# Loading half of k through another queue in fp32, moving the first loads forward, and transposing exponentials as 32-bit words

## The chip, the core and the metric

The kernel runs on one NeuronCore of a Trainium2 chip. A core has a matrix engine (TensorE, PE in the profile, with its weight loads as PEld), a vector engine (VectorE, DVE), a scalar engine (ScalarE, ACT), a general engine (GpSimd, POOL) and a sequencer that issues transfers (SyncE, SP). Each engine works through its own instructions in order; semaphores tie the engines together. Transfers between device memory and the on-chip memory SBUF are issued from SP, ACT or POOL and carried out by 16 DMA engines; matmul results land in eight banks of PSUM. The metric is the device time of one execution in microseconds, as the median of several runs.

## The reference, cut to what matters

```python
def sm_attn(qq, kk, vv):                      # per batch and head
    s = scale * (qq @ kk.T); s = s - s.max(-1)
    a = exp(s); a = a / (a.sum(-1) + 1e-9)
    return a @ vv
p_packed = sm_attn(p, k, v)                   # 32 x 576 scores, per head
x = sm_attn(q, p_packed, p_packed)            # 576 x 32 scores, per head
x = x as [batch, 576, 8 heads * 64]           # then, per batch:
W = (x @ w_q) @ (x @ w_k).T / 8               # 576 x 576
out = relu(W @ x) @ w_out
```

There are 8 batches, 8 heads, 576 positions, 64 channels a head and 32 packed queries p. All tensors are fp32 in device memory; the kernel computes its matmuls in bf16.

## The kernel before, in words

The whole work is unrolled for the eight batches. The string `ORDER` is a list of steps written out by hand, and each engine gets its instructions in the order in which the steps stand there. A step is written `name.batch.part=banks@engine`: `S1.2=2,3,6,7` is the first score product of batch 2 into those PSUM banks, `X1.2.0@A` is an exponential on ACT. `WARM.n` issues n matmuls of 128x512 on a zeroed tile whose result nobody reads; they stand in PE's own order like any other matmul.

For each batch the steps are these. `LD` loads k, q and v; POOL issues these loads, and they turn fp32 into bf16 on the way. `KT` and `QV` (DVE, line 246) transpose k and q in 32x32 blocks of 32-bit words, so that two neighbouring bf16 numbers move as one word. `S1` forms the scores of p with k (lines 282 and 292), `X1` their exponentials (lines 300 and 303), `TE` transposes them on DVE (batches 2 to 7 only; for batches 0 and 1, listed in `DIAG`, S1 gives them already turned), `PV` multiplies them with v and a column of ones (line 323), `RC` and `PP` divide, `PT` transposes the result. `S2`, `X2`, `RS`, `RR`, `AM`, `AT`, `AE` are the second attention, `QK` to `MX` and `MR` the mixing, `RL` the ReLU, `OT` the output product (line 548), `OE` its copy out of PSUM and `ST` the store.

The head of the kernel is what the change touches most. `LD.E0` and `LD.E1` load p of batches 0 and 1 in fp32 (`p32`), one from SP and one from ACT; `EC` on ACT casts both to bf16 in one copy, `EX` on DVE transposes them, and four `PB` copies place them in a block-diagonal operand for S1 of batch 0; three run on DVE, `PB.0.0` on POOL. `LD.F` loads the first 128 rows of the output weights in fp32 from SP into an output buffer that is free then, and `FC` casts them on ACT into `wout`; `LD.O` later brings the other 384 rows through POOL, casting on the way. `LD.h0` and `LD.g0` load the second and the first half of k of batch 0 through POOL. `SET.v` fills the columns of ones beside v, and the loads of v stand behind them.

POOL's loads have eight semaphores to report their landing, used in turn. A load that takes up a semaphore again waits until the load eight places before it has landed, so at most eight are under way.

The exponentials of a batch from 2 on live in `e1T`, which X1 fills in two calls. The call for part cc covers two PSUM banks (the two values of x) of 288 scores; TE transposes the same part in 32x32 blocks of bf16 numbers.

Of the kernel before, what the change touches and what calls it, by code (L numbers as in the profile page):

```python
# [63 lines left out]
def kernel(  # L64
# [64 lines left out]
    def copy(eng, o, i):  # L129
        if eng == "A":  # L130
            nc.scalar.activation(o, i, COPY)  # L131
        elif eng == "P":
            nc.gpsimd.tensor_copy(o, i)
        else:
            nc.vector.tensor_copy(o, i)
# [20 lines left out]

    def load(x, eng):
        a, b = x[0], x[1:]
        if a in "gh":
            i = "gh".index(a)  # L160
            nc.gpsimd.dma_start(k_in[0][:, i], pairs(k, 0)[:, i])
        elif a == "P":
            c = int(b)
            src = p.rearrange("b (i c) (y l) d -> c (b i) y (l d)", i=2, y=2)
            nc.gpsimd.dma_start(pbf[quarter(c)], src[c])
        elif a == "E":
            b = int(b)
            src = p[b].rearrange("(i c) l d -> (c l) i d", i=2)
            (nc.sync if eng == "S" else nc.scalar).dma_start(p32[:, 2 * b:2 * b + 2], src)
        elif a == "W":  # L170
            w = (moe_w_k, moe_w_q)[int(b)].rearrange("(i c j e) m -> (c j) i (e m)", i=2, c=4, e=2)
            nc.gpsimd.dma_start(wqk[:, :, int(b)].rearrange("a i e m -> a i (e m)"), w)
        elif a == "O":
            nc.gpsimd.dma_start(wout[:, 1:], moe_w_out[P:].rearrange("(j a) n -> a j n", a=P))
        elif a == "F":
            nc.sync.dma_start(T["o"][0][:, 0], moe_w_out[0:P])
        elif a == "v":
            b = int(b)
            for i in range(2):
                src = v[b, 4 * i:4 * i + 4].rearrange("c (g r) d -> g c (r d)", r=R)  # L180
                nc.gpsimd.dma_start(v_bufs[b % NL][halves(i), 0:7:2], src)  # L181
        elif a == "k":
            b = int(b)
            nc.gpsimd.dma_start(k_in[b % NL], pairs(k, b))
        elif a == "r" or x in ("q0", "q7"):
            b, i = int(b), int(a == "q")
            nc.gpsimd.dma_start(q_in[b % NL][:, i], pairs(q, b)[:, i])
        else:
            b = int(b)
            nc.gpsimd.dma_start(q_in[b % NL], pairs(q, b))  # L190
# [54 lines left out]
    def blocks(o, i):  # L245
        nc.vector.transpose(o, i)  # L246
# [26 lines left out]
    def S1(b, eng, bk):  # L273
        kT = T["kT", b]
        if b in DIAG:
            z, dz = bk[0], bk[1] - bk[0]
            ps = ps_all[:, z]
            T["s1", b] = bass.AP(ps.tensor, ps.offset, [ps.ap[0], [dz * 512, 3], [1, 384]])
            for r in range(R):
                for e in range(2):  # L280
                    for i in range(2):
                        nc.tensor.matmul(ps_all[halves(i), bk[r // 3], r % 3 * P:(r % 3 + 1) * P],  # L282
                                         kT[:, i, r, :, e],
                                         pblk[:, 2 * b + i, :, :, e].rearrange("a c l -> a (c l)"),
                                         start=e == 0, stop=e == 1, skip_group_check=True)
            return
        T["s1", b] = [ps_all[:, n:n + 2, 0:NT] for n in (bk[0], bk[2])]
        for e in range(2):
            for z in range(4):
                for c in range(4):  # L290
                    i, gh = (c + z) // 2 % 2, (c + z) % 2
                    nc.tensor.matmul(T["s1", b][c // 2][quarter(2 * i + gh), c % 2],  # L292
                                     pT[quarter(c), 2 * b + i, :, e],
                                     kT[quarter(c), i, :, gh * 32:(gh + 1) * 32, e],
                                     start=e == 0, stop=e == 1)

    def X1(b, cc, eng, bk):
        if b in DIAG:
            e1 = new("e1", b, [P, R, C, 2, L], bufs=NE)
            nc.scalar.activation(e1.rearrange("a (z r) c x l -> a z (r c x l)", z=3), T["s1", b], EXP, scale=scale)  # L300
            return
        e1T = new("e1T", b, [P, C, 2, NT], bufs=1)
        nc.scalar.activation(e1T[:, cc], T["s1", b][cc], EXP, scale=scale)  # L303

    def TE(b, cc, eng, bk):
        e1 = new("e1", b, [P, R, C, 2, L], bufs=NE)
        if cc == 2:
            blocks(e1.rearrange("a r c x l -> a (c x) r l"),
                   T["e1T", b].rearrange("a c x (r m) -> a (c x) r m", r=R))
            return  # L310
        blocks(e1[:, :, cc].rearrange("a r x l -> a x r l"),
               T["e1T", b][:, cc].rearrange("a x (r m) -> a x r m", r=R))

    def PV(b, c, eng, bk=None):
        if bk:
            T["pv", b] = ps_all[:, bk[0]:bk[1] + 1, 0:3 * Dh]
        vt = v_bufs[b % NL]
        for n in range(5 * c, min(5 * c + 5, R)):
            for cc in range(C):
                for i in range(2):  # L320
                    rhs = vt[halves(i), 4 * cc:4 * cc + 3, n * Dh:(n + 1) * Dh]
                    lhsT = T["e1", b][halves(i), n, cc].rearrange("a x l -> a (x l)")
                    nc.tensor.matmul(T["pv", b][halves(cc), i], lhsT, rhs, start=n == 0,  # L323
                                     stop=n == R - 1, skip_group_check=True)

# [274 lines left out]
    steps = dict(EC=EC, FC=FC, EX=EX, PX=PX, PB=PB, KT=KT, S1=S1, X1=X1, TE=TE, PV=PV, RC=RC, PP=PP,  # L600
                 PT=PT, QK=QK, QKE=QKE, QD=QD, QV=QV, S2=S2, X2=X2, HA=HA, RS=RS, RR=RR, AM=AM,
                 AT=AT, AE=AE, WKQ=WKQ, WE=WE, GM=GM, GE=GE, Y=Y, YE=YE, MX=MX, MR=MR, RL=RL, RLF=RLF,
                 RLR=RLR, OT=OT, OE=OE, OEF=OEF, ST=ST, STF=STF,
# [49 lines left out]
```

## Time and profile before

| | us |
|---|---|
| median of three runs (lowest, highest) | 107.18 (106.27, 107.47) |
| the profiled execution | 107.46 |
| its span in the trace | 105.4 |
| PE busy in the span | 95.4 |
| DVE busy | 78.2 |
| ACT busy | 65.4 |
| POOL busy | 47.0 |

The span is the time from the first to the last instruction that the profiler saw; some 2.1 us of the execution lie around it. Busy times are sums over instructions, and PE's contain the WARM matmuls. The granted clock of PE was 0.995 of full speed over the span. A group's row in the profile gives line, engine, operation, output and inputs, shapes and count, then the busy time of the group and the mean of one in ns, then the idle time ahead of it and what ended that. A row of the timeline begins with the start and the length of a group of equal instructions in us. The DMA share is the mean busy share of the 16 DMA engines; overlapping packets let it pass 1, and GB/s counts the bytes written.

### The profile page before, as it was taken

What the parts mean: (1) busy time and instruction counts of PE and PEld (TensorE: products, weight loads), DVE (VectorE), ACT (ScalarE), POOL (GpSimd) and SP (SyncE); (2) the same over time, 40 slices, a digit from 0 to 9 for tenths busy, and PEclk for the clock granted to TensorE, in tenths of its full rate; (3) what the DMA queues carried; (4) which work ended last, traced back from release to release, by engine and by line L of the source; (5) the groups of instructions that cost most, each with busy time, mean ns of one, the idle gap of its engine ahead of it and who ended that gap; (6) DMA issues with size and microseconds to landing.
All of it is one profiled execution on the core that took longest, in us unless ns stands there. A gap on an engine that the chain in (4) does not pass through costs nothing.

```text
span 105.4 us, 3620 instructions
## 1 busy us (share of the span) xinstructions
PE 95.4 (91%) x1550; PEld 52.2 (50%) x1550; DVE 78.2 (74%) x150; ACT 65.4 (62%) x108; POOL 47.0 (45%) x76
## 2 busy tenths in 40 slices
PE   3992999798999999999999999999999999999930
PEld 1341645464644654654547536575466654643410
DVE  3615083999798989888898998989997989768000
ACT  5210405043657957879989898598997885556640
POOL 5899540843874226221046459915747019000000
PEclk9999999999999999999999999999999999999997
DMA  2999999999999999999999999999999999868693
GB/s 71 190 185 209 209 202 204 212 207 212 205 211 213 205 207 213 212 211 207 213 213 206 219 200 210 214 206 214 238 342 390 402 401 392 359 239 341 247 339 121
DMA packets 14095, 25.00 MB, mean 237 GB/s; under 512 B 2176, under 2 KB 6912, under 8 KB 14080
## 3 DMA queue, kind: packets, MB, share of 16 engines
q0 software_dynamic: 10176, 15.99, 81.6%
q1 hardware_dynamic: 3488, 8.59, 21.1%
q8 instruction: 12, 0.20, 0.7%
q10 hardware_dynamic: 416, 0.20, 0.7%
q14 instruction: 3, 0.02, 0.1%
HBM read 30.28 MB, written 9.44 MB: 377 GB/s over the span
## 4 chain that ended last, share of the span: by engine, by line
PE 59%; DVE 13%; DMA 10%; POOL 7%; ACT 3%; issue 3%; ACTq 0%; POOLq 0%; DVEq 0%
PE ps L548 26%; DMA k_sb<-in_k_dram 10%; DVE rs L402 4%; PE ps L381 4%; PE ps L323 4%; PE ps L620 4%; PE ps L500 3%; PE ps L427 3%; PE ps L454 3%; PE ps L449 3%; DVE kT L246 2%; DVE a L413 2%; PE ps L475 2%; POOL a L413 2%; PE ps L344 2%
## 5 line engine op out<-in xcount | busy, mean ns | idle before, releaser
L548 PE MATMUL ps<-wout,relu 128*128 128x512 bf16 x124 | 30.7, 380 | 0.0
L620 PE MATMUL ps<-o 128*128 128x512 bf16 x82 | 21.9, 405 | 1.8 <-DVE o L138 1.8
L413 POOL TENSOR_TENSOR a<-e,rr 128x1024 bf16<-128x1024 f32 (+2 forms) x10 | 12.5, 1266 | 18.5 <-DVE rr L407 18.5
L131 ACT ACTIVATE o<-ps 128x1024 f32<-128x1024 f32 (+2 forms) x18 | 15.2, 858 | 4.7 <-PE ps L548 4.7
L548 PEld LDWEIGHTS <-relu 128*128 128x128 bf16 x124 | 10.8, 98 | 11.9 <-issue 2.2
L386 ACT ACTIVATE e<-ps 128x256 f32<-128x256 f32 (+2 forms) x19 | 11.1, 620 | 7.8 <-PE ps L381 7.5
L246 DVE STREAM_TRANSPOSE kT<-k_sb 128x1152 uint32<-128x1152 uint32 (+1 forms) x9 | 11.1, 1235 | 4.6 <-DMA k_sb<-in_k_dram 4.6
L620 PEld LDWEIGHTS <-o 128*128 128x128 bf16 x82 | 7.6, 103 | 10.7 <-issue 2.7
L181 POOL DMA_DIRECT2D v_sb<-in_v_dram x16 | 10.1, 634 | 5.7 <-DMA k_sb<-in_k_dram 2.1
L402 DVE TENSOR_REDUCE rs<-e 128x16 f32<-128x512 f32 (+2 forms) x13 | 10.9, 844 | 1.4 <-ACT e L386 1.2
L511 ACT ACTIVATE relu<-ps 128x1024 bf16<-128x1024 f32 (+1 forms) x12 | 11.1, 954 | 0.6 <-PE ps L506 0.6
L246 DVE STREAM_TRANSPOSE qT<-q_sb 128x1152 uint32<-128x1152 uint32 (+1 forms) x10 | 11.1, 1107 | 0.0
L246 DVE STREAM_TRANSPOSE e<-e1T 128x576 bf16<-128x576 bf16 x12 | 8.7, 745 | 0.6 <-ACT e1T L303 0.6
L131 ACT ACTIVATE wkq<-ps 128x448 bf16<-128x448 f32 (+1 forms) x10 | 7.1, 732 | 2.9 <-PE ps L454 2.2
L303 ACT ACTIVATE e1T<-ps 128x576 bf16<-128x576 f32 x12 | 7.4, 650 | 1.6 <-PE ps L292 1.6
L323 PE MATMUL ps<-v_sb,e 64*64 64x192 bf16 x288 | 7.5, 245 | 0.0
L300 ACT ACTIVATE e<-ps 128x1152 bf16<-128x1152 f32 x2 | 2.3, 1132 | 8.4 <-PE ps L282 8.4
L381 PEld LDWEIGHTS <-qT 64*128 64x128 bf16 x320 | 5.5, 94 | 2.8 <-DVE qT L246 1.6
L323 PEld LDWEIGHTS <-e 64*64 64x64 bf16 x288 | 5.8, 106 | 1.9 <-ACT e L300 1.0
L454 PE MATMUL ps<-aT,pqk 128*128 128x256 bf16 (+1 forms) x48 | 6.8, 246 | 0.0
L381 PE MATMUL ps<-ppT,qT 64*128 64x64 bf16 x320 | 6.4, 190 | 0.3 <-DVE qT L246 0.2
L190 POOL DMA_DIRECT2D q_sb<-in_q_dram x6 | 4.3, 714 | 4.7 <-DMA q_sb<-in_q_dram 2.7
(78 smaller groups left out, 144.4 us busy)
## 6 DMA issues: line engine op xcount, KB each, us to landing
out_dram<-o SPq DMA_DIRECT2D x11, 512.0 KB, 5.3
v_sb<-in_v_dram POOLq DMA_DIRECT2D x16, 288.0 KB, 10.6
k_sb<-in_k_dram POOLq DMA_DIRECT2D x7, 576.0 KB, 12.0
q_sb<-in_q_dram POOLq DMA_DIRECT2D x6, 576.0 KB, 13.7
out_dram<-o SPq DMA_DIRECT2D x5, 256.0 KB, 2.4
q_sb<-in_q_dram POOLq DMA_DIRECT2D x4, 288.0 KB, 9.9
out_dram<-o POOLq DMA_DIRECT2D x2, 512.0 KB, 13.7
out_dram<-orem SPq DMA_DIRECT2D x4, 256.0 KB, 5.1
```

The costliest lines, as they stand in the source:

```text
L131: nc.scalar.activation(o, i, COPY)
L181: nc.gpsimd.dma_start(v_bufs[b % NL][halves(i), 0:7:2], src)
L246: nc.vector.transpose(o, i)
L323: nc.tensor.matmul(T["pv", b][halves(cc), i], lhsT, rhs, start=n == 0, stop=n == R - 1, skip_group_check=True)
L381: nc.tensor.matmul(ps[:, y, t - t0, i], lhsT, rhs, start=e == 0, stop=e == 1)
L386: nc.scalar.activation(e2[:, t0:t1].rearrange("a t (i y n) -> a y (t i) n", i=2, y=2), T["s2", b, c].rearrange("a y t i n -> a y (t i) n") ...
L402: nc.vector.tensor_reduce(rs[:, t0 * H:t1 * H], src, axis=AX, op=ADD)
L413: e.tensor_tensor(a2[:, t0:t1].rearrange("a t i (u l) -> a (t i u) l", l=L), e2v(b, c), T["rr", b][:, t0 * H:t1 * H].to_broadcast((P, (t1 ...
L454: nc.tensor.matmul(o, pqk[:, i, Dl:], aT[:, i, c0:c1], start=i == 0, stop=i == 1)
L511: nc.scalar.activation(o, i, RELU)
L548: nc.tensor.matmul(ps, lhsT, wout[:, j, :], start=j == 0, stop=j == NJ - 1)
L620: nc.tensor.matmul(ps, warm[:, 0:P], warm, start=True, stop=True)
```

## The change

The change has three parts.

The first half of k of batch 0 no longer goes through POOL. It is loaded in fp32 by SP (`LD.H`), as SP's first transfer, into the output buffer where the output weights' rows lay before, and ACT casts it into `k_sb` (`HC`, in `FC`'s place). E0 moves to ACT's queue and E1 to SP's, behind H. POOL begins with the second half of k (`LD.g0`), then v and q of batch 0; the column of ones for v of batch 0 is set by DVE at the very start, and that for batch 3 by POOL after these loads.

The output weights come in one POOL transfer of all 512 rows, at the place of the former `LD.O`; `LD.F` and `FC` are gone.

The exponentials of batches 2 to 7 are stored with the two values of c next to each other, so that a pair is one 32-bit word. S1 writes its four score blocks to the same four banks, two of them exchanged; X1 reads the two banks of its part alternately, one element of each, and writes the pairs; TE transposes 288 words a call instead of 576 bf16 numbers; PV reads its weights with a step of two.

```diff
-LD.E0@S LD.E1@A LD.F@S SET.pz0@V SET.aT0@V SET.warm@V SET.tab@A EC@A FC@A EX@V SET.v1@V SET.idf@V PB.0.2@V LD.h0
-SET.v3@P LD.g0 SET.v0@P LD.v0 LD.q0 SET.mask@P PB.0.0@P PB.0.3@V KT.0.1@V KT.0.0@V PB.0.1@V
+LD.H@S LD.E0@A LD.E1@S SET.v0@V SET.pz0@V SET.aT0@V SET.warm@V SET.tab@A EC@A HC@A EX@V SET.v1@V SET.idf@V PB.0.2@V
+LD.g0 LD.v0 LD.q0 SET.v3@P SET.mask@P PB.0.0@P PB.0.3@V KT.0.1@V KT.0.0@V PB.0.1@V
...
-        if a in "gh":
-            i = "gh".index(a)
-            nc.gpsimd.dma_start(k_in[0][:, i], pairs(k, 0)[:, i])
+        if a == "g":
+            nc.gpsimd.dma_start(k_in[0][:, 1], pairs(k, 0)[:, 1])
...
-            nc.gpsimd.dma_start(wout[:, 1:], moe_w_out[P:].rearrange("(j a) n -> a j n", a=P))
-        elif a == "F":
-            nc.sync.dma_start(T["o"][0][:, 0], moe_w_out[0:P])
+            nc.gpsimd.dma_start(wout, moe_w_out.rearrange("(j a) n -> a j n", a=P))
+        elif a == "H":
+            nc.sync.dma_start(h32, pairs(k, 0)[:, 0])
...
+    h32 = T["o"][0].rearrange("a t n -> a (t n)")[:, 0:RQ * Dh]
...
-    def FC(eng, bk):
-        copy(eng, wout[:, 0], T["o"][0][:, 0])
+    def HC(eng, bk):
+        copy(eng, k_in[0][:, 0], h32)
...
-                    nc.tensor.matmul(T["s1", b][c // 2][quarter(2 * i + gh), c % 2],
+                    nc.tensor.matmul(T["s1", b][c % 2][quarter(2 * i + gh), c // 2],
...
-        e1T = new("e1T", b, [P, C, 2, NT], bufs=1)
-        nc.scalar.activation(e1T[:, cc], T["s1", b][cc], EXP, scale=scale)
+        e1T = new("e1T", b, [P, 2, NT, C], bufs=1)
+        nc.scalar.activation(e1T[:, x], T["s1", b][x].rearrange("a c m -> a m c"), EXP, scale=scale)
...
-        blocks(e1[:, :, cc].rearrange("a r x l -> a x r l"),
-               T["e1T", b][:, cc].rearrange("a x (r m) -> a x r m", r=R))
+    def TE(b, x, eng, bk):
+        e1 = new("e1", b, [P, R, C, 2, L], bufs=NE).rearrange("a r c x l -> a r (c x l)").bitcast(u32)
+        blocks(e1[:, :, x * L:(x + 1) * L],
+               T["e1T", b][:, x].rearrange("a m c -> a (m c)").bitcast(u32).rearrange("a (r m) -> a r m", r=R))
+
+    def e1_of(b, i, n, cc):
+        e1 = T["e1", b][halves(i), n]
+        if b in DIAG:
+            return e1[:, cc].rearrange("a x l -> a (x l)")
+        return e1.rearrange("a c x l -> a (c x l)").rearrange("a (m c) -> a m c", c=C)[:, :, cc]
...
-                    lhsT = T["e1", b][halves(i), n, cc].rearrange("a x l -> a (x l)")
+                    lhsT = e1_of(b, i, n, cc)
```

More of the change, by code (lines that the diff above doesn't have):

```diff
@@ L295, in S1, with X1 @@
                                      start=e == 0, stop=e == 1)
-    def X1(b, cc, eng, bk):
+    def X1(b, x, eng, bk):
         if b in DIAG:
@@ L301, in X1 @@
             return
-        e1T = new("e1T", b, [P, C, 2, NT], bufs=1)
[L303 to L310, printed above, removed]
-        blocks(e1[:, :, cc].rearrange("a r x l -> a x r l"),
-               T["e1T", b][:, cc].rearrange("a x (r m) -> a x r m", r=R))
+        e1T = new("e1T", b, [P, 2, NT, C], bufs=1)
[9 more added lines that the diff above has]
+        return e1.rearrange("a c x l -> a (c x l)").rearrange("a (m c) -> a m c", c=C)[:, :, cc]
     def PV(b, c, eng, bk=None):
@@ L598, in STF @@
         q.dma_start(orows(b)[:, :, t * D:(t + 1) * D], T["o", b][:, t])
-    steps = dict(EC=EC, FC=FC, EX=EX, PX=PX, PB=PB, KT=KT, S1=S1, X1=X1, TE=TE, PV=PV, RC=RC, PP=PP,
+    steps = dict(EC=EC, HC=HC, EX=EX, PX=PX, PB=PB, KT=KT, S1=S1, X1=X1, TE=TE, PV=PV, RC=RC, PP=PP,
                  PT=PT, QK=QK, QKE=QKE, QD=QD, QV=QV, S2=S2, X2=X2, HA=HA, RS=RS, RR=RR, AM=AM,
```

## The prediction

> **What bounds the kernel now.** I read the windows first, to see which engine is full at what time.
>
> ```profile
> span 105.4 us, 3620 instructions
> ...
> 10.00:20.00 10.00, 9.06 (x144) 4.93 (x146) 4.61 (x11) 2.49 (x4) 4.52 (x9) 1.00 1.19 206
> 20.00:30.00 10.00, 9.70 (x185) 6.18 (x182) 9.18 (x25) 4.51 (x9) 5.83 (x11) 1.00 1.14 209
> 30.00:38.00 8.00, 7.70 (x162) 4.08 (x160) 7.48 (x17) 5.40 (x11) 4.11 (x6) 1.00 1.15 208
> 46.00:58.00 12.00, 11.50 (x244) 7.00 (x245) 10.40 (x18) 10.95 (x19) 3.64 (x5) 1.00 1.14 211
> 58.00:70.00 12.00, 12.00 (x256) 6.63 (x256) 11.60 (x20) 9.76 (x15) 7.96 (x12) 1.00 1.15 211
> 10.00:101.20 91.20, 89.08 (x1529) 49.80 (x1529) 73.94 (x139) 62.43 (x103) 38.68 (x55) 1.00 1.08 247
> ```
>
> The columns are PE, weight loads, DVE, ACT, POOL, clock, DMA share, GB/s. From 10 us to 101.2 us PE is busy 89.08 of 91.20 us, so it stands still for 2.1 us in all: 0.94 in 10 to 20, 0.30 in 20 to 30, 0.30 in 30 to 38, 0.50 in 46 to 58, and none in 58 to 70. Part of this work is filler (the WARM steps), but the filler is a fixed number of matmuls in PE's own order, so PE cannot run ahead of it. The time is therefore the start of the first real matmul, plus a fixed PE load, plus 2.1 us of standstill, plus a tail that the change leaves alone. Only the start and the standstill can shrink. Next, PE's waits and the chain:
>
> ```profile
> PE ps L282 <- DVE o L135: 1.9, 1, 1.9
> PE ps L282 <- DVE kT L246: 0.6, 1, 0.6
> PE ps L344 <- DVE ppT L246: 0.3, 1, 0.3
> ```
>
> ```profile
> 7.61 10.76 DMA k_sb<-in_k_dram
> 18.39 1.38 DVE kT L246
> ```
>
> The 1.9 us is the wait ahead of the first S1. The 0.6 and 0.3 both hang on one landing: k of batch 1, issued at 7.61, releases DVE at 18.39; DVE then works without a break until the 0.3 us wait. The head in order of time:
>
> ```profile
> 1.29 0.73 POOL L161 DMA_DIRECT2D k_sb<-in_k_dram  x1 [0.82 <-POOLq L637]
> ...
> 1.83 6.37 PE L620 MATMUL ps<-o 128*128 128x512 bf16 x21 [1.83 <-DVE o L138]
> ...
> 3.11 0.42 ACT L131 ACTIVATE o<-o 128x256 bf16<-128x256 f32 x1 [0.34 <-DMA o<-in_p_dram]
> ...
> 3.94 0.54 DVE L214 MEMSET v_sb<- 128x576 uint32 x1
> ...
> 4.66 0.62 DVE L135 COPY o<-o 32x256 bf16<-32x256 bf16 x2
> ...
> 5.13 0.63 ACT L131 ACTIVATE wout<-o 128x512 bf16<-128x512 f32 x1 [1.60 <-DMA o<-in_moe_w_out_dram]
> ...
> 7.60 0.78 DVE L246 STREAM_TRANSPOSE kT<-k_sb 128x576 uint32<-128x576 uint32 x1 [2.33 <-DMA k_sb<-in_k_dram]
> 8.98 0.78 DVE L246 STREAM_TRANSPOSE kT<-k_sb 128x576 uint32<-128x576 uint32 x1 [0.60 <-DMA k_sb<-in_k_dram]
> 9.79 0.22 DVE L135 COPY o<-o 32x256 bf16<-32x256 bf16 x1
> 10.06 1.24 PE L282 MATMUL ps<-o,kT 128*64 128x128 bf16 x36 [1.86 <-DVE o L135]
> ```
>
> The first load on POOL (second half of k) releases DVE at 7.60, the second (first half) at 8.98, so one 288 KB load of POOL's stream takes 1.38 us. PE starts at 10.06.
>
> **The change part by part.** *1. First S1.* Two conditions must both be met.
>
> ```profile
> o<-in_moe_w_out_dram SPq DMA_DIRECT2D x1, 256.0 KB, 3.8
> ```
>
> ```profile
> 2.00:2.50 0.50, 0.50 (x2) 0.15 (x1) 0.00 (x0) 0.50 (x1) 0.50 (x2) 1.00 1.09 259
> 2.50:3.00 0.50, 0.50 (x2) 0.15 (x1) 0.00 (x0) 0.26 (x2) 0.50 (x2) 1.00 0.94 325
> 3.50:4.00 0.50, 0.50 (x3) 0.21 (x2) 0.37 (x2) 0.03 (x1) 0.20 (x2) 1.00 0.67 95
> 9.00:9.50 0.50, 0.00 (x0) 0.00 (x0) 0.50 (x1) 0.00 (x0) 0.50 (x2) 1.00 1.21 207
> ```
>
> (a) p. E1 now stands behind H on SP, 576 KB in front of 64 KB, and EC waits for both halves of p. No row shows such a queue. Low end: at 325 GB/s from 2.0 us, the stretch in which transfers are seen to flow, 640 KB (655,360 bytes) take 2.0 us, landing at 4.0 and EC at 4.3. High end: the old output row needed 3.8 us for 256 KB beside POOL's stream; H and E1 at that pace, 2.5 times as much, take 9.5 us from 0.76, EC at 10.3. Nearest is the output row itself (released at 5.13 with E0's 64 KB in front, 320 KB on this queue); 320 KB more at 400 GB/s, twice 207 since POOL's loads read four bytes for each two written, are 0.8, so EC at about 5.9, less a little for the earlier issue: I take 5.8. From EC to the end of the two PB copies is 5.28 - 3.11 = 2.17, then two transposes of 0.78, the last PB and its hand-over 0.27: EC plus 4.0, hence 9.8.
> (b) The half that stays on POOL has the first place, issued at 1.29 as before. It shares the DMA engines with 704 KB (H and p) where it was 384 KB (old output row and p): at 400 GB/s up to 0.8 us later than 7.60, or up to 0.6 earlier, if the output row's 256 KB were what held the first load up and H is out of the way by then. I take 7.9. Two transposes and PB give 9.75.
> So S1 starts at 9.8, **0.25 earlier** (ends: 8.8, where WARM is over, see below, and 14.3).
>
> HC, the cast, is not on this path: 0.42 for 256 and 0.63 for 512 elements make 1.16 for 1152, so it runs from 6.2 to 7.4; the transpose that needs it starts at about 8.7. That cover is 1.3 us; beyond it each microsecond delays S1 by one. SET.v0 ahead of the warm memset delays WARM by 0.54, to 2.4; its 6.37 us end at 8.7, 1.1 before S1. POOL sheds one 0.73 us issue and a 0.60 us memset, and issues v and q of batch 0 at once; then PB.0.0 waits for EX, near 6.5, and r0, k1, W1 and W0 queue behind it. Before, they went out from 7.07; they go out about then again, while three loads still wait in the stream: no starvation.
>
> *2. Batch 1 and the standstill.* POOL's stream has lost a load (1.38) and its head is 0 to 0.8 later, so k of batch 1 comes 0.6 to 1.4 earlier; I take 1.0: 17.4. The window 3.50 to 4.00 moved 95 GB/s where 207 is usual, a hole that H fills, which is why I stay above 0.6.
> The Trainium skill, "DMA: Bandwidth & Descriptors", section "Issuing engines are not separate DMA queues", says that issuing from another engine saves the sequencer's time alone, because all transfers share the same 16 DMA engines. By that only the 256 KB output row, leaving the head, would count: 0.6 instead of 1.0, and the time 0.2 higher; the 95 GB/s window speaks for some more.
> With k1 1.0 earlier its transpose ends at 18.8; PE, 0.25 earlier, is ready at 18.95: the wait of 0.6 goes. What is late next is PE's own order. The 0.3 us wait goes too, as DVE's run moves by 1.0 and PE by about 0.9. Sum: **0.25 + 0.6 = 0.85, nearly 0.9 behind the second wait**; I count 0.9.
>
> *3. Output weights in one transfer.*
>
> ```profile
> 26.56 0.74 POOL L174 DMA_DIRECT2D wout<-in_moe_w_out_dram  x1
> 40.12 3.69 PE L548 MATMUL ps<-wout,relu 128*128 128x512 bf16 x16
> 47.22 0.71 POOL L190 DMA_DIRECT2D q_sb<-in_q_dram  x1 [1.94 <-DMA q_sb<-in_q_dram]
> 48.13 1.34 DVE L246 STREAM_TRANSPOSE qT<-q_sb 128x1152 uint32<-128x1152 uint32 x1
> ```
>
> 128 KB more in the stream are 1.38 x 128/288 = 0.6 us. It is covered: the stream is 1.0 ahead there and the first use is 13.6 us after the issue. Behind it the stream is only 0.4 ahead, while PE is 0.9 ahead: the slack of q of batch 3, released at 47.22 and used at 48.13, shrinks from 0.9 to 0.4. Still covered: nothing; without it, up to 0.5.
>
> *4. Exponentials as words.*
>
> ```profile
> L246 DVE STREAM_TRANSPOSE e<-e1T 128x576 bf16<-128x576 bf16 x12 | 8.7, 745 | 0.6 <-ACT e1T L303 0.6
> L323 PEld LDWEIGHTS <-e 64*64 64x64 bf16 x288 | 5.8, 106 | 1.9 <-ACT e L300 1.0 <-issue 0.7 <-DVE e L246 0.2
> L303 ACT ACTIVATE e1T<-ps 128x576 bf16<-128x576 f32 x12 | 7.4, 650 | 1.6 <-PE ps L292 1.6
> L131 ACT ACTIVATE o<-ps 128x1024 f32<-128x1024 f32 x12 | 12.2, 1024 | 3.5 <-PE ps L548 3.5
> L511 ACT ACTIVATE relu<-ps 128x1024 bf16<-128x1024 f32 x10 | 10.0, 1026 | 0.0
> L344 PEld LDWEIGHTS <-ppT 64*64 64x64 bf16 x64 | 2.0, 106 | 1.8 <-DVE ppT L246 1.2 <-issue 0.4
> L246 DVE STREAM_TRANSPOSE ppT<-pp 128x128 uint32<-128x128 uint32 x8 | 2.5, 309 | 0.2
> ```
>
> A TE transposes 288 words instead of 576 halves. 128 words take 309 ns and 576 took 780: 1.05 ns a word, so 288 take about 477, 0.27 less than 745, twelve times 3.2 us of DVE. But PE is the full engine: this buys part of the 0.8 us of standstill in 30 to 58, I say **0.3** (from 0 to 0.8). PV's weights now lie two apart; those of QK do already, and cost 106 like the adjacent ones: nothing. X1 reads PSUM with a step of a whole bank at each element; the ReLU steps 1 KB at every other one and costs 1026 against 1024 for a plain copy, so I take 650 unchanged. Low end 650; high end twice that, as no row shows a step from bank to bank.
>
> **Sum:** 0.9 + 0.3 = 1.2. The profiled execution took 107.46 (its span of 105.4 and 2.1 around it): 106.3. It lies 0.28 above the median of 107.18, so the forecast is **106.0**.
>
> **The rivals.** *p late but absorbed.* If EC comes at 7.0, S1 starts at 11.0, 0.9 later. The 1.24 us of standstill up to 30 us absorb this, since k1 still comes early, and 0.3 remain won by TE: 106.6 to 106.9. The first output row's 3.8 us for 256 KB speak for it; that H is first on SP speaks against. With EC at 8.2 (S1 2.1 later) it is 107.8; the turn is at EC 7.6, and only from EC 8.7 on is it slower by over 1%.
> *Slower: the bank step on ACT.* If X1 doubles, ACT gets 0.65 x 2 a batch for six batches, 7.8 us. In 46 to 58 ACT is busy 10.95 of 12 us, so 1.3 more does not fit; it decides from about 0.5 us a read pair on. Some 0.5 to 0.8 a batch, four crowded batches, less the 1.2 won: 108.6. The relu row speaks against it. The Trainium skill, "SBUF — State Buffer", section "Door 1: The DMA port swizzle (why `[64,N]` ≈ `[32,N]`)", states 8-byte lines in PSUM and a slowdown of matmuls for any access that is not contiguous; the 1026 against 1024 shows none on ACT.
> *More than expected:* p and k both near their good ends, S1 at 9.0, the standstill to 30 us gone but for 0.3, TE 0.5: 1.0 + 0.9 + 0.5 = 2.4: 104.8.
> *The edits do nothing:* the stream refills the gap and only bytes count; S1 unchanged, k1 0.6 earlier, TE hidden: 106.6, in the first rival's band.
>
> **How the numbers follow.** Forecast 0.50 (105.4 to 106.6), absorbed or nothing 0.22 (106.4 to 107.7), more 0.16, bank step 0.09, p very late (EC after 8.7) 0.03. I cut the range at 104.7 and 107.5, leaving out the bank step and half of the outer ends. One per cent (1.07 us, about what a measurement of this kernel tells from no change) puts the edge at 106.1: faster 0.33 of the forecast's 0.50 plus 0.16, 0.49; slower 0.09 plus 0.02 of the very late, 0.11; the rest 0.40.
>
> **What would show it.** EC starting near 5.8 and the first S1 near 9.8; the kT transpose of batch 1 near 17.4 and no PE wait on it; e1T transposes near 477 ns with ACT's X1 at 650; PV weight loads at 106; no PE wait on wout. The prediction is wrong if EC starts after 7.6, if X1 costs over 900 ns, or if PE finds new waits on q or k after 40 us.

## The result, and the profile after

The changed kernel takes 106.42 us (median of 20 runs, 105.39 to 107.16), the kernel before 106.91 us (20 runs beside it, 106.00 to 107.47). The ratio is 0.9933 with a 95% interval of 0.9905 to 0.9961: a gain of 0.7%. The ratio takes only runs within 1.5% of their kernel's fastest, which leaves out four of the 20 runs of the changed kernel and none of the kernel before, while over all runs the medians differ by 0.49 us and the means by 0.52. So the gain is 0.5 to 0.7 us, where 1.2 were forecast. It lies inside the one per cent that the prediction called hard to tell from no change, though the interval does not reach 1. The profiled execution took 106.69 us, with a span of 104.9.

The timeline of the changed kernel's head and of the places where the prediction expected a gain (start and length in us, engine, line, operation, tiles, and in brackets the idle time before it and what ended it):

```profile
2.44 6.51 PE L622 MATMUL ps<-o 128*128 128x512 bf16 x21 [2.44 <-DVE o L138]
...
5.01 0.42 ACT L131 ACTIVATE o<-o 128x256 bf16<-128x256 f32 x1 [2.25 <-DMA o<-in_p_dram]
5.33 1.15 ACT L131 ACTIVATE k_sb<-o 128x1152 bf16<-128x1152 f32 x1
...
6.71 0.71 POOL L183 DMA_DIRECT2D k_sb<-in_k_dram  x1
...
8.61 1.44 DVE L246 STREAM_TRANSPOSE kT<-k_sb 128x576 uint32<-128x576 uint32 x2 [1.60 <-DMA k_sb<-in_k_dram]
...
10.35 1.24 PE L282 MATMUL ps<-o,kT 128*64 128x128 bf16 x36 [1.41 <-DVE o L135]
...
17.05 1.38 DVE L246 STREAM_TRANSPOSE kT<-k_sb 128x1152 uint32<-128x1152 uint32 x1
...
19.42 1.23 PE L282 MATMUL ps<-o,kT 128*64 128x128 bf16 x36
...
24.48 0.64 PE L346 MATMUL ps<-wqk,ppT 64*64 64x128 bf16 x16 [0.30 <-DVE ppT L246]
...
100.05 0.60 PE L587 MATMUL ps<-wout,relu 128*128 128x256 bf16 x4
```

p is early (EC at 5.01, forecast 5.8), and HC takes the 1.15 us that were estimated. But POOL's half of k reaches DVE only at 8.61, so the first S1 begins at 10.35: 0.29 later than before, not 0.25 earlier. k of batch 1, whose load goes out at 6.71 instead of 7.61, is there 1.34 earlier (17.05 against 18.39), and the second S1 starts without a wait, 0.40 earlier (19.42 against 19.82). The 0.30 us wait ahead of QK is still there. From here on the lead hardly moves: 0.43 at QK, and 0.48 at the end of PE (100.65 against 101.13).

The wait ahead of QK stays because DVE now waits for PE. A row of DVE's timeline in the changed kernel:

```profile
23.06 0.17 DVE L329 RECIPROCAL rec<-ps 128x2 f32<-128x2 f32 x1 [0.92 <-PE ps L325]
```

DVE stands idle for 0.92 us until PE has finished PV of batch 1. The division, the transposes and QK follow from that, so an earlier DVE moves nothing.

The groups of the exponentials (the columns are busy us and mean ns of one, then the idle time ahead):

```profile
L246 DVE STREAM_TRANSPOSE e<-e1T 128x288 uint32<-128x288 uint32 x12 | 5.1, 446 | 0.7 <-ACT e1T L303 0.6
...
L303 ACT ACTIVATE e1T<-ps 128x576 bf16<-128x576 f32 x12 | 7.4, 650 | 1.6 <-PE ps L292 1.6
...
L325 PEld LDWEIGHTS <-e 64*64 64x64 bf16 x288 | 5.8, 107 | 1.9 <-ACT e L300 1.0 <-issue 0.9
```

A transpose takes 446 ns instead of 745, 3.6 us less on DVE in all. X1 takes 650 as before although each element now comes from the other bank, and the weight loads of PV with a step of two take 107 against 106.

POOL's and DVE's rows for q of batch 3:

```profile
47.61 0.71 POOL L189 DMA_DIRECT2D q_sb<-in_q_dram  x1 [1.97 <-DMA q_sb<-in_q_dram]
47.68 1.34 DVE L246 STREAM_TRANSPOSE qT<-q_sb 128x1152 uint32<-128x1152 uint32 x1
```

POOL's next load waits for this q, so POOL's row marks its landing. Read so, the slack of this q fell from 0.91 (47.22 to 48.13) to 0.07. Forecast was 0.4. The row comes late, however: in the three traces in which DVE itself waits for this q (transposes swapped; swapped, fillers first; v and q later), POOL's row starts 0.26 us after DVE's. Both slacks are larger by about that much, and the loss of 0.84, where 0.5 was forecast, stays.

### The profile page after: what moved, and what is told of

It is laid out like the page before. It is cut to its first block, busy times and chain, and to the rows that moved or that the text cites. A ratio compares the mean times of both kernels' runs of the same rounds, so it can differ in the third digit from the quotient of the medians.

```text
span 104.9 us, 3598 instructions
## 1 busy us (share of the span) xinstructions
PE 93.5 (89%) x1528; PEld 52.2 (50%) x1550; DVE 75.1 (72%) x151; ACT 65.8 (63%) x108; POOL 45.9 (44%) x74
## 4 chain that ended last, share of the span: by engine, by line
PE 67%; DVE 9%; DMA 7%; ACT 5%; issue 4%; POOL 3%; DVEq 0%; POOLq 0%; ACTq 0%
PE ps L550 26%; PE ps L622 8%; DMA k_sb<-in_k_dram 7%; PE ps L325 6%; PE ps L383 5%; PE ps L502 4%; PE ps L429 3%; PE ps L456 3%; PE ps L451 3%; POOL a L415 3%; DVE rs L404 3%; PE ps L282 2%; PE ps L477 2%; PE ps L346 2%; PE ps L292 2%
## 5 line engine op out<-in xcount | busy, mean ns | idle before, releaser
L550 PE MATMUL ps<-wout,relu 128*128 128x512 bf16 x113 | 29.4, 380 | 0.7 <-issue 0.2
L622 PE MATMUL ps<-o 128*128 128x512 bf16 x73 | 20.3, 410 | 2.9 <-DVE o L138 2.4
L515 DVE TENSOR_SCALAR relu<-ps 128x1024 bf16<-128x1024 f32 (+1 forms) x6 | 6.0, 1034 | 0.5 <-PE ps L502 0.5
```

Source lines behind the costliest of these rows:

```text
L550: nc.tensor.matmul(ps, lhsT, wout[:, j, :], start=j == 0, stop=j == NJ - 1)
L622: nc.tensor.matmul(ps, warm[:, 0:P], warm, start=True, stop=True)
```

## The experiments

Three questions stand behind them. My theory after the result: the first S1 is bound by POOL's half of k, the second by PE's own order, and later the stream of POOL's loads takes back what is won. The rivals: the queue does not matter and only the bytes in the head do; and a single trace does not stand for its kernel at all.

### How far a single trace stands for its kernel

Both kernels were traced once more without any edit.

> The kernel before once more, unaltered. Its first half from POOL was transposed at 7.60 in one execution; in the kernel with the words alone, whose head is the same, at 5.73. If that is the spread of executions, the value here lies between these, the second half near 8.7 to 9.0, the first S1 at 9.8 to 10.1, and k of batch 1 at 17.8 to 18.4.

> The changed kernel once more, unaltered, for a second trace of it. If a trace stands for its kernel to 0.2 us, POOL's half of k is transposed at 8.4 to 8.8, the first S1 starts at 10.2 to 10.5 and k of batch 1 is transposed near 17.0. If the head differs from execution to execution by as much as the times do (105.4 to 107.2), these move by up to 1 us, and only what is the same in both traces can be laid to the change.

The kernel before, second trace:

```profile
1.83 7.62 PE L620 MATMUL ps<-o 128*128 128x512 bf16 x21 [1.83 <-DVE o L138]
9.83 1.23 PE L282 MATMUL ps<-o,kT 128*64 128x128 bf16 x36 [0.38 <-DVE o L135]
...
6.30 0.78 DVE L246 STREAM_TRANSPOSE kT<-k_sb 128x576 uint32<-128x576 uint32 x1 [1.28 <-DMA k_sb<-in_k_dram]
8.48 0.78 DVE L246 STREAM_TRANSPOSE kT<-k_sb 128x576 uint32<-128x576 uint32 x1 [1.40 <-DMA k_sb<-in_k_dram]
...
16.83 1.38 DVE L246 STREAM_TRANSPOSE kT<-k_sb 128x1152 uint32<-128x1152 uint32 x1 [0.36 <-DMA k_sb<-in_k_dram]
...
22.54 0.17 DVE L327 RECIPROCAL rec<-ps 128x2 f32<-128x2 f32 x1 [0.60 <-PE ps L323]
...
18.89 1.24 PE L282 MATMUL ps<-o,kT 128*64 128x128 bf16 x36
```

The changed kernel, second trace:

```profile
2.44 7.31 PE L622 MATMUL ps<-o 128*128 128x512 bf16 x21 [2.44 <-DVE o L138]
9.68 1.24 PE L282 MATMUL ps<-o,kT 128*64 128x128 bf16 x36
...
7.05 1.44 DVE L246 STREAM_TRANSPOSE kT<-k_sb 128x576 uint32<-128x576 uint32 x2
8.52 0.31 DVE L135 COPY o<-o 32x256 bf16<-32x256 bf16 x1
...
16.24 1.33 DVE L246 STREAM_TRANSPOSE kT<-k_sb 128x1152 uint32<-128x1152 uint32 x1
...
18.75 1.23 PE L282 MATMUL ps<-o,kT 128*64 128x128 bf16 x36
```

The landings of one and the same kernel differ by 1.3 to 1.6 us: k of batch 1 is transposed from 18.39 or from 16.83 in the kernel before, POOL's half of k from 8.61 or from 7.05 in the changed one. In its second trace the kernel before has no wait of 0.6 ahead of the second S1 at all; it had been a property of an execution that took 107.46, at the top of that kernel's range (106.00 to 107.47). And in the changed kernel DVE is done at 8.83, but the fillers end at 9.75 and hold the first S1 back to 9.68 (ends of PE are modelled). The 21 fillers took 6.37 us in the first trace and 7.62 here.

Two sums give the start of the second S1. Without a wait it comes 9.07 after the first (10.35 to 19.42, 9.68 to 18.75); with a wait it comes 1.43 after DVE begins with k of batch 1 (18.39 to 19.82). The later of the two decides: so it comes out within 0.02 us in eleven of the 14 traces of this study. The other three are the one with five fillers fewer, which shortens the first sum, and two with swapped transposes, in which the second S1 comes 8.94 and 8.95 after the first without a wait. The table is read from the same rows of each trace's timeline:

| trace | last half of k | fillers end | first S1 | k of batch 1 | second S1 | QK of batch 1 to end of PE |
|---|---|---|---|---|---|---|
| before | 8.98 | 8.20 | 10.06 | 18.39 | 19.82 | 76.22 |
| before, again | 8.48 | 9.45 | 9.83 | 16.83 | 18.89 | 76.21 |
| words alone | 8.68 | 8.21 | 9.84 | 18.00 | 19.43 | 76.16 |
| changed | 8.61 | 8.95 | 10.35 | 17.05 | 19.42 | 76.17 |
| changed, again | 7.05 | 9.75 | 9.68 | 16.24 | 18.75 | 76.18 |
| head alone | 8.65 | 9.83 | 10.39 | 16.96 | 19.46 | 76.42 |
| transposes swapped | 8.41 | 10.01 | 9.94 | 16.89 | 18.88 | 76.56 |
| v and q later | 7.55 | 9.58 | 9.50 | 16.36 | 18.57 | 76.72 |
| five fillers fewer | 8.02 | 9.59 | 9.89 | 16.65 | 18.21 | 76.51 |
| swapped, fillers first | 8.22 | 7.98 | 9.05 | 17.39 | 18.83 | 76.33 |
| the same, fewer output weights | 8.31 | 7.83 | 9.14 | 16.65 | 18.09 | 76.48 |
| both halves by POOL | 7.27 | 9.23 | 9.16 | 15.72 | 18.22 | 76.16 |
| by POOL, again | 7.75 | 8.82 | 8.98 | 17.33 | 18.77 | 76.26 |
| by POOL, fillers first | 7.80 | 8.79 | 8.99 | 17.43 | 18.86 | 76.32 |

"Last half of k" is the start of the transpose that had to wait for a landing last; where two transposes form one row, it is the start of that row, and a second transpose follows it. In the two rows that join swapped transposes and early fillers, the first matmul of the first S1 ran at 8.10 and 8.02, and the time in the table is that of the other 35.

### Words alone, head alone

Words alone is the kernel before with the new S1, X1, TE and PV; head alone is the changed kernel with those four put back.

```diff
-                    nc.tensor.matmul(T["s1", b][c // 2][quarter(2 * i + gh), c % 2],
+                    nc.tensor.matmul(T["s1", b][c % 2][quarter(2 * i + gh), c // 2],
...
-        blocks(e1[:, :, cc].rearrange("a r x l -> a x r l"),
+        blocks(e1[:, :, x * L:(x + 1) * L],
```

> The kernel before with the exponentials as words alone (S1, X1, TE and PV as changed; loads, casts and order as before). Theory A (the start of the first S1 and PE's own order set the time, DVE's relief lies beside a full PE): TE at 446 ns instead of 745, the first S1 at 10.0 to 10.1 as before, time within 0.15 us of the kernel before. Rival B (DVE is the second bound of the middle stage, and its 3.6 us are what shortened the changed kernel): 0.4 to 0.6 us faster than before.

> The changed kernel without the words (TE on bf16 as before; H, the new order of loads and the output weights in one transfer kept). Theory A: the first S1 at about 10.35, the second S1 near 19.4, time 0.3 to 0.5 us below the kernel before. Rival B: the head's loss of 0.3 at the first S1 is not made good, time 0 to 0.3 above the kernel before.

Words alone: 106.80 us, ratio 0.9979 (0.9946 to 1.0011), not told apart from no change. Head alone: 106.44 us, ratio 0.9952 (0.9909 to 0.9995). The two gains, 0.2% and 0.5%, add up to the 0.7% of the whole, but their intervals are as wide as the gains. The time alone does not decide on the words either: the interval still holds the rival's 0.4 to 0.6 us.

The traces price the words more finely, by the last column of the table, the time from QK of batch 1 to the end of PE. In the kernel before it is 76.22 and 76.21, with the words 76.16, 76.17 and 76.18: they are worth 0.05 us here, for 3.6 us less on DVE. That is no more than the spread of this column, which reads 76.16, 76.26 and 76.32 in the three traces with the words and a head by POOL. In the one trace with the new head and the old exponentials it is 76.42, so with that head they may be worth 0.25; one trace does not settle it.

### Which queue brings the first half of k

Both halves go through POOL in bf16 again, the second half first; p is back on its two queues; the words and the single transfer of the output weights stay.

```diff
-LD.H@S LD.E0@A LD.E1@S SET.v0@V SET.pz0@V SET.aT0@V SET.warm@V SET.tab@A EC@A HC@A EX@V SET.v1@V SET.idf@V PB.0.2@V
-LD.g0 LD.v0 LD.q0 SET.v3@P SET.mask@P PB.0.0@P PB.0.3@V KT.0.1@V KT.0.0@V PB.0.1@V
+LD.E0@S LD.E1@A SET.v0@V SET.pz0@V SET.aT0@V SET.warm@V SET.tab@A EC@A EX@V SET.v1@V SET.idf@V PB.0.2@V
+LD.g0 LD.H LD.v0 LD.q0 SET.v3@P SET.mask@P PB.0.0@P PB.0.3@V KT.0.1@V KT.0.0@V PB.0.1@V
...
-            nc.sync.dma_start(h32, pairs(k, 0)[:, 0])
+            nc.gpsimd.dma_start(k_in[0][:, 0], pairs(k, 0)[:, 0])
```

> The changed kernel with both halves of k of batch 0 through POOL again in bf16, the second half first; p is back on the two queues it had, and nothing is cast on ACT but p. It tells the queue apart from the bytes, since the 256 KB of output weights are gone from the head in both. If the DMA engines are shared whoever issues, k of batch 1 reaches DVE at the same time as in the changed kernel (17.1 to 17.4), and the first half of POOL's k lands near 7.6 as it did before the change. If SP's queue fills time that POOL's stream leaves empty, k of batch 1 comes later, by up to the 1.38 us of one half: 17.8 to 18.6. In both cases the second of the halves lands near 9.0 and the first S1 starts at 10.0 to 10.2; PE ends at 100.5 to 101.0 and the time is 106.4 to 106.9.

> The version with both halves of k through POOL once more, unaltered. If the transfer of H in fp32 is what holds POOL's stream up in the changed kernel, the two halves are transposed at 5.4 to 6.5 and 7.0 to 7.8 again, k of batch 1 at 15.5 to 16.5, and q of batch 3 is there about 1 us before the 47.6 of the changed kernel. If it was luck of one execution, k of batch 1 is at 17 or later.

106.41 us, ratio 0.9965 (0.9937 to 0.9994). The first trace of it:

```profile
9.16 1.24 PE L282 MATMUL ps<-o,kT 128*64 128x128 bf16 x36
...
5.62 0.78 DVE L246 STREAM_TRANSPOSE kT<-k_sb 128x576 uint32<-128x576 uint32 x1 [0.26 <-DMA k_sb<-in_k_dram]
7.27 0.79 DVE L246 STREAM_TRANSPOSE kT<-k_sb 128x576 uint32<-128x576 uint32 x1 [0.87 <-DMA k_sb<-in_k_dram]
...
15.72 1.32 DVE L246 STREAM_TRANSPOSE kT<-k_sb 128x1152 uint32<-128x1152 uint32 x1
```

The second trace:

```profile
8.98 1.23 PE L282 MATMUL ps<-o,kT 128*64 128x128 bf16 x36 [0.17 <-DVE o L135]
...
7.75 0.78 DVE L246 STREAM_TRANSPOSE kT<-k_sb 128x576 uint32<-128x576 uint32 x1 [0.66 <-DMA k_sb<-in_k_dram]
...
17.33 1.38 DVE L246 STREAM_TRANSPOSE kT<-k_sb 128x1152 uint32<-128x1152 uint32 x1 [1.70 <-DMA k_sb<-in_k_dram]
```

The expectation of 9.0 for the second half and of 10.0 to 10.2 for the first S1 fell: POOL alone has both halves there at 7.3 to 7.8, and the first S1 at 8.98 to 9.16, earlier than any trace of the changed kernel (9.68 and 10.35) or of the head alone (10.39). k of batch 1 comes no later without SP's transfer: 15.72, 17.33 and 17.43 in the three traces by POOL (mean 16.8), 17.05, 16.24 and 16.96 with the first half by SP (mean 16.8), 18.39, 16.83 and 18.00 with the old head (mean 17.7). The four other traces with the first half by SP and v and q issued as in the changed kernel have 16.65 to 17.39. By what was expected of the second trace, the 15.72 of the first was luck of one execution. So the 1 us that k of batch 1 gained does not come from the other queue. What both new heads share is that the 256 KB of output weights and their cast are gone from the head; to remove them alone was not tried. They share a second thing: POOL has less to do ahead of the load of k of batch 1 (DVE sets the ones of v of batch 0), and this load goes out at 6.39 to 6.76 in the eleven traces with a new head, at 7.61 in the three with the old one. That is 0.85 to 1.22 earlier, as much as it lands earlier on the mean, and no run changes the one without the other. So which of the two brings k of batch 1 forward is not shown. That the queue does not decide it is what the rule in the Trainium skill, "DMA: Bandwidth & Descriptors", section "Issuing engines are not separate DMA queues", says, and these traces agree with it in the kind of the effect: moving a transfer to SP bought no transfer time (means of 16.8 and 16.8).

### v and q of batch 0 issued later

```diff
-LD.g0 LD.v0 LD.q0 SET.v3@P SET.mask@P PB.0.0@P
+LD.g0 SET.v3@P SET.mask@P LD.v0 LD.q0 PB.0.0@P
```

> The changed kernel, but POOL sets the ones of v of batch 3 and the mask before it issues v and q of batch 0, so that these loads go out about 1.5 to 2 us later. The half of k on POOL landed 7.3 us after its issue (6.3 before the change), its transpose began at 8.61. If it is v and q, now close behind, that share the engines with it, it lands at 7.6 to 8.0 and the first S1 starts at 9.4 to 9.8. If it is H and p in the head that slow it, it stays at 8.4 to 8.8 and the first S1 at 10.1 to 10.4; k of batch 1 is 0 to 0.5 us later than 17.05 in either case. The time: 106.2 to 106.7.

106.24 us, ratio 0.9967 (0.9941 to 0.9993). POOL's half of k was transposed from 7.55 and the first S1 began at 9.50, which fits the case that v and q slow that half; but the unaltered kernel had 7.05 in its second trace, so it proves nothing. k of batch 1 was transposed from 16.36, not 0 to 0.5 later than 17.05, although v went out 1.4 us later than in the changed kernel (3.40 against 2.02); this one trace speaks against the earlier issue of v and q as what brings it forward. The waits of DVE show what it costs later (us in total, times, longest):

```profile
DVE qT L246 <- DMA q_sb<-in_q_dram: 1.2, 2, 0.8
```

Two q came late, by 0.8 and 0.4 us, and the stretch to the end of PE was 0.55 longer than in the changed kernel (76.72 against 76.17).

### The order of the two transposes, and the start of the fillers

First the order alone: the half that ACT casts is transposed first.

```diff
-PB.0.3@V KT.0.1@V KT.0.0@V PB.0.1@V
+PB.0.3@V PB.0.1@V KT.0.0@V KT.0.1@V
```

> The changed kernel with one edit in the order: DVE takes the last PB copy and the transpose of the SP half of k first, and the transpose of the POOL half last. Theory A: the half from POOL, released near 8.6, is what the first S1 waits for; with one transpose of 0.75 left behind it, S1 starts at 9.4 to 9.6 instead of 10.35 and the time falls by 0.5 to 0.9 below the changed kernel, 1.0 to 1.4 below the kernel before. Rival C (the first S1 has 0.5 or more of slack, because DVE's chain behind k of batch 1 sets PE's later start): S1 starts earlier, the stretch behind it is lost again by 25 us, no more than 0.2 below the changed kernel.

106.53 us, ratio 0.9981 (0.9939 to 1.0023). The first S1 came at 9.94, not at 9.4 to 9.6, and the time shows no gain. PE's timeline and DVE's row for q of batch 3:

```profile
2.44 7.57 PE L622 MATMUL ps<-o 128*128 128x512 bf16 x21 [2.44 <-DVE o L138]
9.94 1.25 PE L282 MATMUL ps<-o,kT 128*64 128x128 bf16 x36
...
47.93 1.38 DVE L246 STREAM_TRANSPOSE qT<-q_sb 128x1152 uint32<-128x1152 uint32 x1 [0.69 <-DMA q_sb<-in_q_dram]
```

The fillers, which the change starts at 2.44 instead of 1.83, are the bound here: they end at 10.01, while DVE is done at 9.19. So the zeroing of their operand was put first, ahead of two memsets that stood before it even in the kernel before, so that the fillers now start at 1.21:

```diff
-SET.v0@V SET.pz0@V SET.aT0@V SET.warm@V SET.tab@A EC@A HC@A
+SET.warm@V SET.v0@V SET.pz0@V SET.aT0@V SET.tab@A EC@A HC@A
```

> The changed kernel with the two k transposes of batch 0 in the other order (the half that ACT casts first) and the zeroing of the filler operand at the very start, as it was before the change. If the first S1 in the swapped kernel was held at 9.94 by the filler matmuls (which started at 2.44 and ended at 10.01), the fillers now start near 1.83 and end between 8.2 and 9.4, and the first S1 starts near 9.3, when the second transpose ends; the second S1 near 18.9 and QK of batch 1 near 23.9. If the stream of POOL's loads caps the gain at q of batch 3, DVE then waits 0.7 us or more for that q, PE ends at 100.4 to 100.6, and the time is only 0.0 to 0.3 below the changed kernel's. Rival, in which the stream does not cap it: the lead of some 0.5 us at QK of batch 1 is still there at the end, PE ends near 100.1, and the time is 0.5 lower. The fillers and the head cannot be the bound if the first S1 stays at 9.9.

106.33 us, ratio 0.9952 (0.9922 to 0.9982):

```profile
1.21 6.77 PE L622 MATMUL ps<-o 128*128 128x512 bf16 x21 [1.21 <-DVE o L138]
...
8.10 0.24 PE L282 MATMUL ps<-o,kT 128*64 128x128 bf16 x1
9.05 1.24 PE L282 MATMUL ps<-o,kT 128*64 128x128 bf16 x35 [0.71 <-DVE kT L246]
...
17.39 1.38 DVE L246 STREAM_TRANSPOSE kT<-k_sb 128x1152 uint32<-128x1152 uint32 x1 [1.83 <-DMA k_sb<-in_k_dram]
...
18.83 1.23 PE L282 MATMUL ps<-o,kT 128*64 128x128 bf16 x36 [0.78 <-DVE kT L246]
...
47.67 1.38 DVE L246 STREAM_TRANSPOSE qT<-q_sb 128x1152 uint32<-128x1152 uint32 x1 [0.50 <-DMA q_sb<-in_q_dram]
...
47.93 0.71 POOL L189 DMA_DIRECT2D q_sb<-in_q_dram  x1 [1.95 <-DMA q_sb<-in_q_dram]
```

All but one matmul of the first S1 run from 9.05, 1.3 before the changed kernel's first trace, and PE then waits 0.78 us for k of batch 1. What the head wins, the next landing takes in this trace. The fillers were a bound, then, and behind them stands the landing of k of batch 1. Whether the stream caps the rest is not decided: DVE waits 0.50 for q of batch 3 (expected 0.7 or more), and PE ends at 100.22, between the 100.4 to 100.6 of a cap and the 100.1 of its rival.

The same step in the version by POOL:

> Both halves of k of batch 0 through POOL in bf16 (second half first), as in the kernel before, p back on its queues, the output weights in one transfer and the exponentials as words as in the changed kernel; and the zeroing of the filler operand at the very start. With the fillers starting at 2.44, the first S1 of the version by POOL began at 9.16, right behind the last filler, while DVE was done at 8.3. If the fillers were its bound, they now start near 1.2 and end near 8, and the first S1 starts at 8.2 to 8.6; the second S1 and all that follows move by what the second wait leaves, 0.3 to 0.9, and PE ends near 98.9 (99.44 with the late fillers): time 0.3 to 0.6 below the changed kernel's. If the early landing of k in that execution (5.4 and 7.0) was luck of one execution, the first S1 is at 9.8 to 10.1 here as in the kernel before.

106.48 us, ratio 0.9955 (0.9922 to 0.9988). The first S1 came at 8.99, not at 8.2 to 8.6: the fillers took 7.58 us this time and ended at 8.79, and the second half of k, transposed from 7.80, held it 0.20 us longer. k of batch 1 was transposed from 17.43, so that the second S1 waited 0.74 us for it. The expected gain did not come.

### Less in the stream behind it

The kernel with swapped transposes and early fillers, with 384 KB less of output weights in POOL's stream. It leaves out three quarters of the output product, so only its time counts:

```diff
-            nc.gpsimd.dma_start(wout, moe_w_out.rearrange("(j a) n -> a j n", a=P))
+            nc.gpsimd.dma_start(wout[:, 0], moe_w_out[0:P])
+            nc.gpsimd.memset(wout[:, 1:].rearrange("a j n -> a (j n)").bitcast(u32), 0)
```

> The kernel with the swapped transposes and the early filler operand, but POOL loads only the first 128 of the 512 rows of the output weights, and sets the other 384 to zero: that part of the output product is left out, so only the time counts. POOL's stream has 384 KB less ahead of q of batch 3; at 1.38 us for 288 KB that is 1.8 us. If the stream is the cap, q of batch 3 lands 1 to 1.8 us earlier, DVE's wait for it goes, and PE ends 0.3 to 0.5 us earlier than with the full load, near 100.1; the time falls by as much. Rival: if q of batch 3 only shows up as the last of several waits (PE full anyway), its wait goes but PE ends within 0.1 us of the kernel with the full load.

105.96 us, ratio 0.9946 (0.9916 to 0.9976). Its median is 0.37 lower than with the full load, its ratio only 0.0006, so the times do not decide. POOL's and DVE's rows:

```profile
45.18 0.71 POOL L190 DMA_DIRECT2D q_sb<-in_q_dram  x1 [2.19 <-DMA q_sb<-in_q_dram]
...
36.19 1.38 DVE L247 STREAM_TRANSPOSE kT<-k_sb 128x1152 uint32<-128x1152 uint32 x1 [0.57 <-DMA k_sb<-in_k_dram]
...
46.68 1.34 DVE L247 STREAM_TRANSPOSE qT<-q_sb 128x1152 uint32<-128x1152 uint32 x1
```

q of batch 3 is there 2.75 us earlier than with the full load (POOL's rows, 45.18 and 47.93), and its wait is gone. But PE now runs so early that DVE waits 0.57 us for k of batch 3, which was issued ahead of the output weights. From QK of batch 1 to the end it takes 76.48, not less than the 76.33 with the full load. In this trace the 0.3 to 0.5 us expected of my theory did not come behind QK; the rival, in which that q is only one of several waits, describes it. That PE ended 0.59 earlier is due to the earlier start (k of batch 1 at 16.65 against 17.39), which the edit cannot have touched.

### Five fillers fewer ahead of the second S1

```diff
-WARM.10=6 S1.1=0,1,2
+WARM.5=6 S1.1=0,1,2
```

> The changed kernel with five of the ten filler matmuls ahead of the second S1 left out. Theory A (PE cannot run ahead of its own fillers: k of batch 1 comes 1.3 earlier but the filler's end sets the second S1): S1 of batch 1 starts near 18.5 instead of 19.42, when its transpose ends, QK of batch 1 about 0.8 earlier, time 0.5 to 0.9 below the changed kernel. Rival C (something else, DVE or POOL, is bound there too): S1 of batch 1 earlier, but QK within 0.2 of 24.48 and no gain.

106.69 us, ratio 0.9956 (0.9920 to 0.9992). The five fillers are 1.07 us of PE (0.214 each), and the second S1 came 8.32 after the first instead of 9.07. PE's timeline, and then one of its waits (us in total, times, longest):

```profile
18.21 1.23 PE L282 MATMUL ps<-o,kT 128*64 128x128 bf16 x36 [0.27 <-ACT e L388]
```

```profile
PE ps L550 <- DMA wout<-in_moe_w_out_dram: 0.3, 1, 0.3
```

PE gains 0.75 (0.27 go to a wait for ACT) and then waits for the output weights themselves, 0.3 us. In its profiled execution (105.83) the rest arrives; the median shows nothing of it. In no run did a version stand out: all ratios lie between 0.993 and 0.998, and their intervals overlap.

## Why the prediction was right or wrong

The time lies in the stated range, but this says little: 104.7 to 107.5 holds the kernel before as well. Of the three terms of the sum, 0.25, 0.6 and 0.3, the first is not seen, the second came in part, though not because a load left POOL's stream, and the third measured 0.05. That the time came within 0.42 us of the forecast is partly luck.

**The bound.** Right: PE is the full engine, its own order carries a lead unchanged, and only the start and the standstill count. The table shows it more sharply than the windows did: where no load behind it is late, QK of batch 1 is followed by 76.16 to 76.42 us, whatever the head did.

**Step 1, the first S1.** Wrong. Part (a) was safe: EC at 5.01, HC 1.15 and covered. Part (b) failed in the release of POOL's half, taken at 7.9: it was 8.61 in the trace compared and 7.05 or earlier in the next. The first S1 moved by +0.29 in the first pair of traces and by -0.15 in the second, so the term of 0.25 is not seen; its mean over the three traces with each head went from 9.91 to 10.14. The second error is the cover of 1.1 us for the later fillers, which rests on 6.37 us as their length. They took 6.38 to 7.62 in later traces, and in the changed kernel's second trace they held the first S1: DVE was done at 8.83, S1 began at 9.68. Of these 0.85 us up to 0.61 (2.44 against 1.83) are the price of `SET.v0` ahead of them, which the prediction had put at nothing.

**Step 2, k of batch 1.** The size is right: 17.05 against a forecast of 17.4, 1.0 earlier on the mean of three traces. Its reason fell: POOL's stream need not lose a load for it, nor H fill a hole, as POOL alone brings that k as early. It also held that the loads behind the head go out at about the same time as before; k of batch 1 went out 0.90 earlier, and this may be the reason. The wait of 0.6 went, but it was the wait of one execution; another of the kernel before has none. That is the term that was mis-sized: between executions it is 0 to 0.6, and was counted whole. The 0.3 us ahead of QK, counted as going, stayed in the changed kernel. By the prediction's own numbers, DVE 1.0 and PE 0.9 earlier, only 0.1 of it would have gone. The prediction saw in it DVE's unbroken work since k of batch 1; in the second trace of the kernel before, where k of batch 1 comes early, DVE waits 0.60 us for PV instead, as it does in the changed kernel.

**Step 3, the output weights in one transfer.** Right that it is covered: PE shows no wait on them in the changed kernel. The slack of q of batch 3 was put at 0.4 and is 0.07 by the same rows; the step before overrated how far the stream stays ahead. The stream was 1.34 ahead at k of batch 1 and 0.39 behind at this q. Of the 1.73 us between, the 128 KB account for 0.6 by the estimate; the rest is not resolved, and the second trace of the kernel before has this q at 47.28 in POOL's row beside a DVE that starts on it at 47.17 without a wait, so that the slack of 0.9 was again that of one execution.

**Step 4, the words.** The three prices were right: 446 ns (estimated 477), X1 at 650, the weight loads at 107. The term of 0.3 is wrong: it measured 0.05 (76.22 to 76.17). PE's waits in the kernel before, from 30 to 38 and from 46 to 58 us, could have told it:

```profile
PE ps L427 <- DVE a L413: 0.2, 1, 0.2
...
PE ps L449 <- DVE aT L135: 0.2, 1, 0.2
PE ps L427 <- POOL a L413: 0.2, 1, 0.2
```

They hang on `a` and `aT` of the second attention; none names the transposed exponentials. I had put the standstill down to DVE as an engine instead of reading which step it waits for. The windows after show it unspent:

```profile
46.00:58.00 12.00, 11.56 (x243) 7.05 (x244) 9.82 (x16) 10.96 (x19) 3.73 (x5) 1.00 1.14 210
```

DVE is busy 0.58 us less than before in these 12 us, PE stands still for 0.44 instead of 0.50. Such sums of PE are a weak witness: the trace after holds 1528 matmuls and that before 1550, beside 1550 weight loads in both, and a matmul without a record reads as standstill (0.57 after against 0.30 before in 30 to 38 us). The last column of the table goes by a start and an end, and is the firmer one.

**The rivals.** The bank step on ACT did not come (650). p was not late. The lower price, k of batch 1 only 0.6 earlier, cannot be told from the 1.0 of the means, as two traces of one kernel differ by up to 1.6.

**What stays open.** Medians and ratio say 0.5 to 0.7 us were gained; three traces of each head say 0.17 at the second S1 (means 19.38 and 19.21), with a spread of 0.9 within one kernel. How much of the gain belongs to the output weights that left the head, and how much to the earlier issue of the loads behind it, the runs do not separate. Why the same loads land up to 1.6 us apart was not found.

## What to carry to other kernels

Before pricing a wait in the head, look whether it is the kernel's or the execution's: trace the kernel twice, since a load's landing moved here by more than the whole effect of the change. A gain at the head reaches the end only as far as the slack of every later landing lets it, so write down for each the later of "PE ready" and "data ready" and take the maximum, as the 9.07 and 1.43 do here. And take work off an engine only where the bound engine's waits name that very work: 3.6 us less on DVE gave 0.05.

## What was unexpected of the hardware

The 21 fillers run at 0.43 us each at first and at about 0.21 later, and when the pace changes differs from execution to execution. The weight loads of PE in the first trace of the kernel before, then in its second (a load every 0.43 us stands by itself, the fast ones form a group):

```profile
1.83 0.13 PEld L620 LDWEIGHTS <-o 128*128 128x128 bf16 x2 [1.83 <-DVE o L138]
...
5.22 2.49 PEld L620 LDWEIGHTS <-o 128*128 128x128 bf16 x12 [0.28 <-issue]
```

```profile
7.36 0.15 PEld L620 LDWEIGHTS <-o 128*128 128x128 bf16 x1 [0.28 <-issue]
7.78 1.18 PEld L620 LDWEIGHTS <-o 128*128 128x128 bf16 x6 [0.27 <-issue]
```

It changed 3.39 us after the first filler in the one and 5.95 us in the other, which are the extremes of the 14 traces. So these 21 fillers last 6.4 to 7.6 us, and a load that is ready earlier waits for them. That the pace is the clock is not shown here: the granted clock of the profile reads 1.00 over the slow fillers too (the row of 2.00 to 2.50 us in the prediction). The Trainium skill, "TensorE: Matmul & The Clock Gate", section "Part 1: The HAM clock gate (the "warmup" mystery)", states a window of about 3.4 us that runs freely, so that the rise of the clock depends on where in it the first matmul falls; 3.39 and 5.95, between about one window and two, agree with that. The 0.5 us either way that it gives for this spread is less than the 2.6 measured here, and the measurement decides.

Reading PSUM with a step of a whole bank cost ACT nothing (650 ns both ways), and loading weights with a step of two cost PE 1 ns in 106.
